# Attention and an MLP mixer on one core: block transposes that read with a step, per-unit moves, and row 0 written by the same list as the other rows

## The chip, the core and the metric

The kernel runs on one core of a Trainium2 chip. The core has five engines that run side by side, each through its own instruction stream in order: TensorE (PE, matrix products, with its weight loads shown apart as PEld), VectorE (DVE), ScalarE (ACT), GpSimd (POOL) and SyncE (SP). They meet only at semaphores. Data moves by DMA; a transfer is issued by an instruction in the queue of one of the engines (here SP's and ScalarE's), carried by 16 DMA engines, and counted as landed when its semaphore is raised. Matrix products land in PSUM, which has eight banks; everything else lives in SBUF, 128 partitions wide.

The metric is the device time of one execution in microseconds (us), the median of several runs.

## The reference

Eight batch rows, eight heads, 576 tokens, head size 64. All arithmetic is in float32. The four weight matrices come as float64 and the kernel turns them into float32 itself.

```python
scores = scale * np.matmul(q, k.transpose(0, 1, 3, 2))
thresh = np.max(scores, axis=-1, keepdims=True) - tau
scores = np.where(scores >= thresh, scores, -1000000000.0)
attn = np.exp(scores - np.max(scores, axis=-1, keepdims=True))
attn = attn / (np.sum(attn, axis=-1, keepdims=True) + 1e-09)
out = np.matmul(attn, v)                       # heads side by side: x is (8, 576, 512)
h = np.maximum(x.transpose(0, 2, 1) @ w_tok1, 0.0) @ w_tok2      # token products, 576 -> 256 -> 576
u = x + h.transpose(0, 2, 1)
return u + np.maximum(u @ w_ch1, 0.0) @ w_ch2                    # channel products, 512 -> 1536 -> 512
```

## The kernel before

**Units and groups.** Attention of a batch row is done for pairs of heads (`p`), two pairs at a time, in 18 units of 128 query rows (`units`; nine units cover two pairs, and unit 4 of the nine takes 64 rows of each, `SHARED`). For a unit, `scores` are products of 128 queries with 576 keys, for two heads. VectorE takes the maximum (`top`, L859), GpSimd makes a bias of it (`shift`, L864), ScalarE cuts what is below the threshold (`mask`, L874, an activation out of PSUM) and takes exponentials with their sum (`exps`, L884), VectorE inverts the sum (`inverse`, L337 and L338), GpSimd scales (`scale`, L345). Then the weights `e` (128 queries by 1152 keys of two heads) must be turned, since the product with v contracts over keys. Three units make a group (`GU`), and one call of `values` (L425, L430) does the product for a group into one PSUM bank, which is copied to `xT`.

**Turning e, rows 1 to 7.** VectorE's transpose works on blocks of 32 x 32. `turn_blocks` (L382) turns a unit's blocks into a part of the tile `T`, one `T` for a group, two in rotation: block row i of the queries stays in partitions 32i to 32i+31, and the four blocks a of every 128 keys lie side by side. `move` then brings block (i, a) from partitions 32i.. to partitions 32a.. by DMA from SP's queue (L392): for each a four transfers, each of 32 partitions for three units at once, 16 transfers for a group, issued when all three units are turned. **u** (the residual input of the channel products) is turned in the same manner for the final addition: `turn_u` (L937) and `move_u` (L944), 16 transfers for a group of 256 tokens; the put-off groups do so too (`Late.turn_u`, L1274 and L1280).

**Turning e, row 0.** TensorE turns 128 x 128 pieces against an identity (`turn`, L363), nine for a unit in three thirds, and VectorE (thirds 0 and 2) or ScalarE (third 1) copies them out of PSUM (`turned`, L369).

**MLP.** A row's token products come in steps x (turn back, L459 and L463), 1 (L471) and 2 (L483, with the sum on VectorE in L493), then channel products for a group of 256 tokens: `ch1` (L950), `ch2` (L966), addition and store. Row 0 does two such groups, rows 1 to 6 one, and what is left of each row is written to DRAM (`spill`, L535) and done at the end in five joined groups (`Late`, L1285), with seven products in place of eight; six sums of weights (`sums`, L1206 and L1209) are made for these on VectorE.

**Order of the work.** Row 0 is a loop written out by hand (`for u in range(UB)`): in each turn the scores of a unit, a value group or an early token step, the scaling of the unit before, a portion of the weight conversion (`weight_to`: 31 pieces, each loaded by L192 and passed through ScalarE, VectorE and GpSimd), and the turning of the unit two back. It has PSUM pools of its own (`ps_tr`, `ps_3rd`, `ps_sc`). From row 1 on the order is planned while the program is built: `Scheduler` holds items with an engine, a cost in us, a lag, a rank and dependences, plays them against one clock for each engine, and writes out whichever can start first. Scores come there in rounds of two units (`make_round`, `scores_of_two`, L846) into two tiles of three banks (`ps_s2`); the other two banks (`ps_b`) serve all else. `planned_at` says how much MLP work is to be done before a round's scores. The loads of q and k (`load_qk`, L108; 72 KB each in rows of 128 bytes, eight for a pair) are issued from SP's queue in row 0 and from ScalarE's queue later, into one buffer each (`lq`, `lk`), and turned by `prep` (L294). The end of the attention and of the last row is:

```python
    sched.run(attention_done)
    attn.close()
```

Of the kernel before, what the change touches and what calls it, by code (L numbers as in the profile page):

```python
# [21 lines left out]
def kernel(  # L22
# [55 lines left out]
    row0 = ctx.enter_context(ExitStack())  # L78
    ps_tr = row0.enter_context(tc.tile_pool(name="ps_tr", bufs=2, space=bass.MemoryType.PSUM))
    ps_3rd = row0.enter_context(tc.tile_pool(name="ps_3rd", bufs=1, space=bass.MemoryType.PSUM))  # L80
    ps_sc = row0.enter_context(tc.tile_pool(name="ps_sc", bufs=2, space=bass.MemoryType.PSUM, side="right"))
# [16 lines left out]
    def load_qk(n, eng, parts=range(8), blocks=(range(S // 32),) * 2):  # L98
# [3 lines left out]
        if n not in loaded:  # L102
            loaded[n] = [att.tile([P, S // 32, 32], F32, tag=tag, bufs=1, name=f"{tag}_{n}") for tag in ("lq", "lk")]
# [22 lines left out]
    FIRST = P // 32  # L126
# [4 lines left out]
    load_qk(0, (nc.sync, None), range(0, 8, 2), (range(FIRST, S // 32), None))  # L131
# [49 lines left out]
    def load_piece(i):  # L181
# [7 lines left out]
        if i == len(pieces) - 2:  # L189
            raw_at[i % NRAW] = work.tile([P, NTK * DM], F32, tag="a", bufs=1, name="spare_a").bitcast(U32)  # L190
# [46 lines left out]
    steps_done = 0  # L237

    def weight(n):

        nonlocal steps_done
        for k in range(steps_done, min(steps_done + n, 3 * len(pieces) + 1)):
            i, part = divmod(k, 3)
            if part == 0:
                on_gpsimd(i - 1)
                if i:
                    load_piece(i - 1 + NRAW)
            else:
                on_scalar(i + 1, part - 1)
            on_vector(i, part)  # L250
            steps_done = k + 1

    def weight_to(x):

        weight(max(int(x) - steps_done, 0))

    def need(i):

        weight(3 * i + 4 - steps_done)

    load_piece(0)
    load_v(0)
    for i in range(1, NRAW):
        load_piece(i)
    load_v(1)

# [24 lines left out]
    def scores(u):  # L298
        b, p0, t = units[u]
        sc = [  # L300
            (ps_3rd if b == 0 and (2 * u + h) % 3 == 2 else ps_sc).tile([P, 2, MAIN], F32, tag="sc", name=f"sc{h}_{u}") for h in range(2)
        ]
        if t == SHARED:
            parts = [(b * NP + p0, slice(MAIN, S), slice(0, 64)), (b * NP + p0 + 1, slice(0, LAST), slice(64, P))]
        else:
            o = P * t if t < SHARED else LAST + P * (t - SHARED - 1)
            parts = [(b * NP + p0 + (t > SHARED), slice(o, o + P), slice(0, P))]
        order = [(f, part, h) for f in range(2) for part in parts for h in range(2)]
        for f, (n, cols, rows), h in order if b else sorted(order, key=lambda o: o[2]):
            r = slice(D * h, D * h + D)  # L310
            qT, kT = heads[n]
            nc.tensor.matmul(sc[h][rows, f, 0:HS], lhsT=qT[r, cols], rhs=kT[r, HS * f : HS * f + HS], start=True, stop=True)
        mx = small.tile([P, 2], F32, tag="mx", name=f"mx_{u}")
        bias = small.tile([P, 2], F32, tag="bias", name=f"bias_{u}")
        for h in range(2):
            c = slice(h, h + 1)
            nc.vector.tensor_reduce(out=mx[:, c], in_=sc[h][:, :, 0:HS], axis=AX.XY, op=ALU.max)
            nc.gpsimd.tensor_scalar(out=bias[:, c], in0=mx[:, c], scalar1=toff, scalar2=-SCALE, op0=ALU.add, op1=ALU.mult)
        st[u] = sc, bias
# [28 lines left out]
    def small_bank(name):  # L348
        return ps_tr.tile([P, MAIN], F32, tag="tr", name=name)
# [1114 lines left out]
```

## Time and profile before

| | us |
|---|---|
| median of 3 runs (1387.57 to 1390.39) | 1389.01 |
| the profiled execution: time | 1385.2 |
| the profiled execution: span, first to last instruction | 1383.4 |
| TensorE busy (mean granted clock 0.965) | 1264.3 |
| VectorE busy | 780.9 |
| ScalarE busy | 563.9 |
| GpSimd busy | 371.5 |
| row 0's first channel product (L950) starts | 165.5 |
| last conversion on GpSimd (L231) starts | 177.9 |
| attention of the last row ends on TensorE | 959.5 |

A "busy" figure is the time in which the engine had an instruction at work. A wait is written as *engine tile line <- who ended it: us in total, times, longest*. An instruction list of a line gives count, shortest, median and longest duration in ns, and first and last start. Letters after an engine (SPq, ACTq) mean its instruction queue, where DMA issues stand. Idle time of an engine that isn't the bound costs nothing by itself.

### The profile page before, as it was taken

What the parts mean: (1) busy time and instruction counts of PE and PEld (TensorE: products, weight loads), DVE (VectorE), ACT (ScalarE), POOL (GpSimd) and SP (SyncE); (2) the same over time, 40 slices, a digit from 0 to 9 for tenths busy, and PEclk for the clock granted to TensorE, in tenths of its full rate; (3) what the DMA queues carried; (4) which work ended last, traced back from release to release, by engine and by line L of the source; (5) the groups of instructions that cost most, each with busy time, mean ns of one, the idle gap of its engine ahead of it and who ended that gap; (6) DMA issues with size and microseconds to landing.
All of it is one profiled execution on the core that took longest, in us unless ns stands there. A gap on an engine that the chain in (4) does not pass through costs nothing.

```text
span 1383.4 us, 21958 instructions
## 1 busy us (share of the span) xinstructions
PE 1264.3 (91%) x7902; PEld 1003.6 (73%) x7902; DVE 780.9 (56%) x1422; ACT 563.9 (41%) x1208; POOL 371.5 (27%) x710
## 2 busy tenths in 40 slices
PE   7882899989898899899989899998999999999998
PEld 5552677758675676775777587676698888888887
DVE  5877866664455755665666566663334344434342
ACT  6775655564544545545544545462011111102020
POOL 4565533333133332333323233330000001010100
PEclk7995999999999999999999999999899999999999
DMA  6436677762777665767666666665011110121011
GB/s 112 108 89 154 165 142 150 134 132 71 155 154 152 141 130 125 166 131 148 137 135 129 136 146 129 138 142 127 1 56 29 59 30 28 32 61 31 31 31 31
DMA packets 310589, 145.15 MB, mean 105 GB/s; under 512 B 210064, under 2 KB 303248, under 8 KB 310480
## 3 DMA queue, kind: packets, MB, share of 16 engines
q1 hardware_dynamic: 182768, 127.84, 40.3%
q10 hardware_dynamic: 127712, 15.90, 8.0%
q8 instruction: 63, 1.03, 0.3%
q14 instruction: 46, 0.38, 0.1%
HBM read 47.32 MB, written 13.50 MB: 44 GB/s over the span
## 4 chain that ended last, share of the span: by engine, by line
PE 59%; DMA 13%; DVE 10%; SPq 10%; ACT 4%; issue 2%; POOL 1%; ACTq 1%; DVEq 0%; POOLq 0%
SPq L392 9%; PE o L1285 9%; PE bank L966 7%; DMA eT<-T 6%; PE sc L846 6%; PE hx L1285 6%; PE bank L430 5%; PE bank L950 5%; PE hmm L1285 4%; PE oz L1285 4%; PE hz L1285 4%; DVE mx L859 3%; PE bank L483 3%; DMA lk<-in_k_dram 2%; PE bank L471 2%
## 5 line engine op out<-in xcount | busy, mean ns | idle before, releaser
L345 POOL TENSOR_SCALAR e<-e,rr 128x576 f32<-128x576 f32 x288 | 213.7, 755 | 303.1 <-DVE rr L338 270.6
L874 ACT ACTIVATE e<-sc,bias 128x576 f32<-128x576 f32 x252 | 173.6, 740 | 237.0 <-DVE mx L859 119.4
L859 DVE TENSOR_REDUCE mx<-sc 128x1 f32<-128x576 f32 x252 | 173.9, 748 | 61.9 <-PE sc L846 61.2
L382 DVE STREAM_TRANSPOSE T<-e 128x1152 f32<-128x1152 f32 x126 | 171.2, 1364 | 41.4 <-POOL e L345 19.9
L884 ACT ACTIVATE e<-e,ntau 128x576 f32<-128x576 f32 x252 | 193.0, 777 | 0.8
L950 PE MATMUL bank<-xT,wc 128*128 128x256 f32 x768 | 178.9, 389 | 12.6 <-DVE x_sb L463 7.2
L966 PEld LDWEIGHTS bank<-wc,g 128*128 128x128 f32 x1536 | 175.4, 192 | 8.5 <-issue 3.6
L966 PE MATMUL bank<-wc,g 128*128 128x128 f32 x1536 | 179.8, 276 | 0.2 <-ACT x_sb L463 0.2
L950 PEld LDWEIGHTS bank<-xT,wc 128*128 128x128 f32 x768 | 145.1, 193 | 42.8 <-issue 7.5
L846 PE MATMUL sc<-kT,qT 64*128 64x192 f32 (+1 forms) x1680 | 146.9, 335 | 12.2 <-ACT e L874 12.0
L846 PEld LDWEIGHTS sc<-kT,qT 64*128 64x128 f32 (+1 forms) x1680 | 122.3, 178 | 39.4 <-issue 18.4
L430 PE MATMUL bank<-eT,lv 128*64 128x384 f32 (+1 forms) x912 | 130.6, 430 | 0.0
L1368 POOL TENSOR_TENSOR us<-us,ut 128x256 f32<-128x256 f32 x27 | 22.4, 843 | 401.8 <-DVE us L1206 401.8
L430 PEld LDWEIGHTS bank<-eT,lv 128*64 128x64 f32 x912 | 76.6, 148 | 45.7 <-issue 31.6
L864 POOL TENSOR_SCALAR bias<-mx,toff 128x1 f32<-128x1 f32 x252 | 66.4, 268 | 152.6 <-DVE mx L859 149.2
L483 PE MATMUL bank<-w,a 128*128 128x288 f32 x256 | 70.9, 424 | 12.8 <-DVE xT L493 10.2
L425 PE MATMUL bank<-eT,vl 128*64 128x384 f32 (+1 forms) x228 | 43.8, 462 | 39.6 <-DMA eT<-T 17.5
L483 PEld LDWEIGHTS bank<-w,a 128*128 128x128 f32 x256 | 47.4, 193 | 33.2 <-DVE xT L493 14.6
L471 PE MATMUL bank<-x_sb,w 128*128 128x512 f32 (+1 forms) x170 | 70.8, 567 | 0.5 <-ACT x_sb L463 0.5
L1206 DVE TENSOR_TENSOR temps<-hx,temps 128x256 f32<-128x256 f32 x60 | 25.5, 425 | 63.5 <-PE hx L1285 63.4
L1333 ACT ACTIVATE ga<-hmm 128x256 f32<-128x256 f32 x30 | 11.5, 384 | 117.0 <-PE hmm L1285 117.0
L1285 PE MATMUL hx<-t,wc 128*128 128x256 f32 x240 | 56.7, 379 | 0.0
(147 smaller groups left out, 1685.8 us busy)
## 6 DMA issues: line engine op xcount, KB each, us to landing
eT<-T SPq DMA_DIRECT2D x672, 108.0 KB, 2.4
lv<-in_v_dram SPq DMA_DIRECT2D x32, 288.0 KB, 3.8
out_dram<-us SPq DMA_DIRECT2D x32, 256.0 KB, 2.1
ut<-us SPq DMA_DIRECT2D x256, 32.0 KB, 1.9
lk<-in_k_dram ACTq DMA_DIRECT2D x109, 72.0 KB, 3.3
lq<-in_q_dram ACTq DMA_DIRECT2D x106, 72.0 KB, 2.9
spare<-in_moe_w_ch_dram SPq DMA_DIRECT2D x8, 512.0 KB, 3.8
extra<-in_moe_w_ch_dram SPq DMA_DIRECT2D x8, 512.0 KB, 3.7
```

Source lines behind the costliest of these rows:

```text
L345: nc.gpsimd.tensor_scalar(out=eh, in0=eh, scalar1=rr[:, h : h + 1], scalar2=1.0, op0=ALU.mult, op1=ALU.mult)
L382: nc.vector.transpose(out=T[:, :, place, :].rearrange("p a (c x) -> p c a x", c=NK), in_=e.rearrange("p (c a x) -> p c a x", c=NK, a=4))
L392: nc.sync.dma_start(out=turned_e[key][32 * a : 32 * a + 32, :, i, :], in_=Ts[key][32 * i : 32 * i + 32, a, :, :])
L430: nc.tensor.matmul(to[r], lhsT=lv[:, j, :], rhs=e[j], start=False, stop=(c == NI - 1), skip_group_check=True)
L483: nc.tensor.matmul(bank[:, 0:HS], lhsT=hidden[b][:, m, P * c : P * c + P], rhs=w2[:, m, HS * f : HS * f + HS], start=(m == 0), stop=(m == ...
L846: nc.tensor.matmul(sc[h][rows, f, HT * k : HT * k + HT], lhsT=qT[r, cols], rhs=kT[r, HT * f : HT * f + HT], start=True, stop=True, skip_gr ...
L859: nc.vector.tensor_reduce(out=mx[:, h : h + 1], in_=part[h], axis=AX.XY, op=ALU.max)
L874: nc.scalar.activation(out=eh, in_=part[h], func=AF.Prelu, bias=bias[:, h : h + 1], scale=SCALE, alpha=STEEP)
L884: nc.scalar.activation(out=eh, in_=eh, func=AF.Exp, bias=ntau, accum_out=rs[:, h : h + 1])
L950: nc.tensor.matmul(bank[:, 0:n], lhsT=wc1[:, j, c, :], rhs=uT[:, c, GR * i : GR * i + n], start=(c == 0), stop=(c == NCC - 1))
L966: nc.tensor.matmul(to, lhsT=s["g"][:, j, P * t : P * t + P], rhs=wc2[:, j, P * c : P * c + P], start=(j == 0 and b > 0), stop=(j == NJ - 1 ...
L1285: nc.tensor.matmul(ps, lhsT=l, rhs=r, start=start and x == 0, stop=x == len(pairs) - 1, skip_group_check=not start)
```

## The change

It has three parts.

*Transposes with a step.* VectorE's transpose of a unit now reads, out of every 128 keys, the keys 4r + a (r from 0 to 31) as its block a, where it read the 32 keys from 32a on. After the transpose partition 32i + r holds, for query block i, all four a side by side, which are the keys 4r + a; and so one transfer can bring the 32 partitions of a query block to all 128 partitions of `eT`. There are four transfers for a unit, each 144 KB, issued for every unit by itself; `T` belongs to a unit and has three buffers. `u` is treated in the same way, in the rows (two transfers for each of four blocks) and in the put-off groups (eight for each half).

*Row 0 by the list.* The loop is gone, with its PSUM pools; row 0's units are made by `make_round` like all others, in rounds of two, with the turning by TensorE in three thirds as items of the list. The weight conversion becomes a set of items (`make_conversion`), and so do the token steps of row 0's first half (`make_half_row`).

*Costs and buffers.* Nearly all item costs, ranks and lags get new numbers. Items on SP's queue get a model of transfers: eight in flight, a rate, a landing time. All loads of q and k after the first move to SP's queue, with two buffers; `e` has four buffers, not three; one spare conversion buffer gets a place of its own.

```diff
-            loaded[n] = [att.tile([P, S // 32, 32], F32, tag=tag, bufs=1, name=f"{tag}_{n}") for tag in ("lq", "lk")]
+            loaded[n] = [att.tile([P, S // 32, 32], F32, tag=tag, bufs=2, name=f"{tag}_{n}") for tag in ("lq", "lk")]
...
-            Ts[key] = att.tile([P, 4, GU, NK * 32], F32, tag="T", name=f"T_{u}")
-        T = Ts[key]
-        nc.vector.transpose(
-            out=T[:, :, place, :].rearrange("p a (c x) -> p c a x", c=NK), in_=e.rearrange("p (c a x) -> p c a x", c=NK, a=4)
-        )
+        T = Ts[u] = att.tile([P, 4, NK * 32], F32, tag="T", bufs=3, name=f"T_{u}")
+        nc.vector.transpose(
+            out=T.rearrange("p a (c x) -> p c a x", c=NK), in_=e.rearrange("p (c r a) -> p c a r", c=NK, a=4)
+        )
...
         for i in range(4):
-            nc.sync.dma_start(out=turned_e[key][32 * a : 32 * a + 32, :, i, :], in_=Ts[key][32 * i : 32 * i + 32, a, :, :])
+            nc.sync.dma_start(
+                out=turned_e[key][:, place, i, :], in_=T[32 * i : 32 * i + 32]
+            )
...
-    for u in range(UB):
-        _, p0, t = units[u]
...
-        scores(u)
...
+    FLIGHT, RATE, LANDING = 8, 214.0, 1.5
...
+            if x.dmas and len(self.in_flight) == FLIGHT:
+                t = max(t, self.in_flight[0])
...
-                put(("load", n, lo), sched.op("act", 0.9, lambda lo=lo: load_qk(n, (nc.scalar,) * 2, range(lo, lo + 2)), ahead, 3, lag=3.0))
...
+                    sched.op(
+                        "sp",
+                        0.9,
+                        lambda lo=lo: load_qk(n, (nc.sync,) * 2, range(lo, lo + 2)),
+                        ahead,
+                        0,
+                        after=(key_op("load", n - 1, LOADS - 2),),
+                        dmas=(2, 107, 0.45),
+                    ),
...
-            e = att.tile([P, 2 * S], F32, tag="e", bufs=3, name=f"e_{u}")
+            e = att.tile([P, 2 * S], F32, tag="e", bufs=4, name=f"e_{u}")
...
-        us = (UB + 2 * it, UB + 2 * it + 1)
+        us = (2 * it, 2 * it + 1)
...
-        x.plan = planned_at(row, k)
+        x.plan = planned_at(row - 1, k) if row else -1.0
...
-            if t % GU == 0:
-                deps += [key_op("M", G - 2, a) for a in range(4)] if G >= 2 else [key_op("V", G - 2)]
-            deps.append(key_op("T", u - 1))
-            put(("T", u), sched.op("dve", 1.37, lambda u=u: turn_blocks(u), deps, 4))
+            deps += [key_op("T", u - 1), key_op("M", u - 3)]
+            put(("T", u), sched.op("dve", 1.31, lambda u=u: turn_blocks(u), deps, 4))
+            put(
+                ("M", u),
+                sched.op(
+                    "sp",
+                    2.4,
+                    lambda u=u: move(u),
+                    (key_op("T", u), key_op("V", G - 2) if t % GU == 0 else None),
+                    0,
+                    after=(key_op("M", u - 1),),
+                    dmas=(4, 147, 0.6),
+                ),
+            )
...
-            for a in range(4):
+            for n in range(2):
                 for k in range(4):
-                    nc.sync.dma_start(out=ut[32 * a : 32 * a + 32, :, k, :], in_=us[32 * k : 32 * k + 32, :, a, :])
+                    nc.sync.dma_start(out=ut[:, n, k, :], in_=us[32 * k : 32 * k + 32, n])
```

## The prediction

> **What bounds the kernel now.** First the busy time of the engines in four stretches (columns: stretch and length, then busy time and instructions of matmul, weight load, VectorE, ScalarE and GpSimd, then clock, DMA share, GB/s).
>
> ```profile
> 0.00:165.50 165.50, 117.62 (x683) 78.78 (x684) 125.35 (x247) 110.44 (x225) 91.03 (x147) 0.85 0.53 124
> 165.50:934.00 768.50, 710.74 (x5106) 546.39 (x5105) 478.80 (x850) 390.22 (x834) 255.20 (x533) 0.98 0.67 138
> 934.00:971.00 37.00, 28.78 (x179) 23.37 (x178) 15.60 (x14) 7.26 (x18) 2.93 (x4) 0.94 0.48 118
> 971.00:1384.00 413.00, 407.18 (x1940) 355.05 (x1940) 161.13 (x313) 56.02 (x133) 22.39 (x27) 0.99 0.13 35
> ```
>
> TensorE is the bound from 165.5 us on (92% in the seven rows, 99% in the put-off groups). Its idle time is 47.9 us at the start, 57.8 in the rows, 8.2 at their end, 5.8 in the last stretch: 119.7 us, and only this, the slow clock that goes with it (0.85 at the start) and any TensorE work dropped can be won. The rows take 768.5/7 = 109.8 us each, 101.5 of them TensorE.
>
> Then, where TensorE waits: its list of waits between 173 and 934 us, and its largest wait after 934.
>
> ```profile
> PE bank L425 <- DMA eT<-T: 17.5, 9, 3.6
> PE bank L425 <- DMA ut<-us: 11.3, 3, 6.7
> PE bank L483 <- DVE xT L493: 9.2, 7, 2.5
> PE bank L950 <- DVE xT L434: 3.1, 1, 3.1
> PE bank L425 <- DVE T L382: 3.1, 1, 3.1
> ...
> PE bank L950 <- DVE x_sb L463: 7.2, 1, 7.2
> ```
>
> L425 is the first matmul of a group's values. It waits for the moves of the turned weights (eT<-T, L392); where the wait is put on ut<-us, SP's queue held the u moves between them. That is 28.8 us, 31.9 with the one on L382, of the row stage's 57.8. The timeline of SP's queue shows the two sharing one line (start, length, instruction):
>
> ```profile
> 359.87 20.58 SPq L392 DMA_DIRECT2D eT<-T  x24
> 380.49 5.08 SPq L944 DMA_DIRECT2D ut<-us  x8
> ...
> 571.31 14.61 SPq L392 DMA_DIRECT2D eT<-T  x16
> ```
>
> One issue takes 598 ns where nothing holds it (instruction list of L392), so sixteen take 9.6 us at best and here 14.6, then 2.4 us to land. Last, ScalarE's waits after 165 us, and the turning instruction:
>
> ```profile
> ACT e L874 <- DMA lk<-in_k_dram: 31.2, 6, 6.7
> ACT e L874 <- DMA lq<-in_q_dram: 22.8, 5, 5.5
> ...
> L382 DVE STREAM_TRANSPOSE T<-e x126: 1334/1369/1380, 144.0 to 940.6; 128x1152 f32<-128x1152 f32 x126
> ```
>
> The q and k loads stand in ScalarE's own queue, and it is held 54 us by them.
>
> **The change, step by step, against the profiled execution (span 1383.4, time 1385.2, so 1.8 around it).** The result is quoted as a median: before's, 1389.0, is 3.8 above the profiled execution, and I add that at the end.
>
> *Moves of e.* 672 issues become 504 (12 for three units, not 16): 168 x 0.598 = 100 us less of SP's queue. The path gets shorter by more than that: after the third unit's transpose there were 16 issues (9.6 us) before the last landing; now units 1 and 2 have gone ahead and 4 remain (2.4 us): 7.2 us earlier, 42 times. Bytes are alike (672 x 108 KB and 504 x 144 KB, 72.6 MB), so the DMA engines win nothing. A shape of 144 KB over 128 partitions isn't in the trace; its landing lies between the 2.4 us of eT (108 KB) and the 3.8 us of lv (288 KB); I take 2.6. The longest wait on these moves is 3.6 us and a wait on ut 6.7, all at or under 7.2, so up to all 31.9 us could go; what is late next is the scaling on GpSimd and L382 itself, and the list starts values earlier where it believes the moves are. I take two thirds, 20 us; bounds 5 (the list only shifts its order) and 32.
>
> *Moves of u.* 96 become 48 in the rows: 8 x 0.595 = 4.8 us less per group, already in the 31.9. The 160 late ones become 80; TensorE is 99% busy there: nothing, the cover is the whole channel phase between transpose and first use.
>
> *Transposes that read with a step.* 126 of L382 now read every fourth element. The bottom is the row's minimum, 1.33 us. No row reads at that step: L223 reads every second word in 691 ns for 512, while contiguous two-input L1209 takes 683, so a step of two is free. Upper end: twice, 2.74 us (an estimate; step four touches twice the length of step two). I take 1.37, nearest to L223, cost nothing: VectorE is busy 68.4 of 109.8 us per row. At 2.74 it would have 93 of 109.8.
> The Trainium skill ("SBUF — State Buffer", section "Door 1: The DMA port swizzle") says memory lines are 16 bytes, that two hits per line are wanted and each access crossing to a new line pays; four fp32 are exactly one line, so it speaks against this read. L223 stays at two hits per line, so no run here shows it. By that rule the transposes would sit towards 2.74 and the sum would lose some 30 us; by the row, none.
>
> *q and k loads from ScalarE's queue to SP's, with two buffers.* 215 issues at 320 to 483 ns leave ScalarE, and its 54 us of waits with them. SP gets 32 a row, 13 us. SP per row: before 96 x 0.598 + 16 x 0.595 x 6/7 + 4 x 0.48 = 67 us plus stores; after 72 x 0.598 + 4.1 + 13 + 1.9 = 62. So its load is no larger, but now moves queue behind loads. Gain on TensorE: of named waits, only 0.9 us on L846 <- ACT: zero, bound -54 (rival 2) to +4.
> By "DMA: Bandwidth & Descriptors", section "Issuing engines are not separate DMA queues", the two queues end on the same 16 DMA engines and a second only saves issue time; that agrees with no gain in transfer, and puts the price on SP alone.
>
> *Row 0 by the list.* In the changed kernel's order of instructions, before row 0's first channel matmul (at 165.5 us in the trace, L950) TensorE gets four rounds of row 1, not three, and the weight conversion ends inside row 0's units. ScalarE's work until there: 25 units x (2 x 0.740 + 2 x 0.977) = 86, 31 pieces x 2 x 0.6 = 37, 26 copies of eT x 0.479 = 12, others 5: 140 us. VectorE: 26 x 2 x 0.748 = 39, conversion 44, copies 28 x 0.55 = 15, preps 12 x 0.75 = 9, reciprocals and the rest 19: 126. Now it is VectorE's 125.4 us in 165.5 (76%). At 90% of ScalarE: 140/0.9 = 156; at 96%, 146; at 80%, 175. I take 90% (TensorE's share in the list's own rows): 10 us gained; bounds -10 and 20. The matmuls of scores in row 0 also change: 31.6 us busy for 18 units (L312) against 146.9/126 x 18 = 21.0 in the form of L846: 10.6 us less TensorE work, but it lies where TensorE is idle anyway; I count 2.
>
> *Last row's end.* The 7.2 us before L950: two x_sb copies stood on VectorE behind six weight sums of 1.76 us (L1206, L1209). In the changed kernel's order all of that row's copies are on ScalarE. Gain 6; bounds 0 and 7.
>
> *Clock.* In the rows the mean is 0.98; after a wait of 3.6 us four matmuls of L425 took 1.55 us, not 0.87. Shorter waits give some of the lost 2% of 711 us back: 3; bounds 0 and 10.
>
> *Item costs and SP's model in the list* have no time of their own; they change which order is written, and are in the two thirds above.
>
> **Sum**: 20 + 10 + 2 + 6 + 3 = 41; span 1383.4 - 41 = 1342, time 1344, median **1348**.
>
> **Rivals.**
> 1. *The moves are hidden anyway, and row 0 gains little.* For: TensorE is at 92%, and a list that plans values earlier may just wait on VectorE's xT sums (L483, 9.2 us) or on evictions instead. Against: 28.8 us of waits carry the moves' name. Then 5 + 0 + 2 + 6 = 13 us, or 23 with the start's 10: median 1366 to 1376.
> 2. *Slower: SP's queue becomes the wait.* Place: a load of q or k at the head of SP's queue, waiting for its buffer or behind a store that waits for its sums, with moves behind it. For: 11 waits of 4.9 us on these loads hit ScalarE now. Price: up to 54 us on values. Against: two buffers let loads run a pair ahead. It decides when over 41 of these 54 us reach TensorE with the 20 us of the moves lost too, from 21 us: 30 to 45 us on TensorE gives 1383.4 - 21 + 30..45, median 1398 to 1413.
> 3. *Slower: step-four transposes at half rate.* 18 x 1.37 = 24.7 us more VectorE a row, to 85%; it becomes the bound outright only above 1.37 + (101.5 - 68.4)/18 = 3.2 us. Before that each value group is 1.4 us later and evictions queue: 4 to 8 us a row against 41 gained: median 1376 to 1404.
> 4. *No change in all:* the gains meet a row 0 that runs at 80%: about 1389.
>
> **How the numbers follow.** Forecast 0.50 (1328 to 1362: start at its bounds, moves 10 to 32); rival 1 0.27; rival 2 0.12; rival 3 0.08, half of it slower; rival 4 0.03. The measurement of before spreads 1387.57 to 1390.39, so 0.2% (2.8 us) is about what can be told. Faster 0.50 + 0.27 + 0.04 (rival 3's milder half) = 0.81; slower 0.12 + 0.04 = 0.16; same 0.03. Range 1324 to 1398: it holds the forecast, rival 1 and the milder half of the slower ones.
>
> **What would show it.** Right: L425's waits on eT<-T under 10 us in the rows, no wait over 2 us on u's moves; ScalarE's waits on lk and lq gone; L382 still at 1.37 us; row 0's first channel matmul near 156 us; no 7 us hole before the last row's token products; row stage near 745 us. Wrong: SP issues of moves waiting behind loads, L382 over 1.8 us, TensorE idle at the start over 50 us, or a new wait on scaling or evictions that takes the place of the moves'.

## The result, and the profile after

| | us |
|---|---|
| before, median of 4 runs (1386.25 to 1390.39) | 1388.29 |
| after, median of 4 runs (1365.39 to 1372.79) | 1369.74 |
| ratio, with its 95% interval | 0.986 (0.983 to 0.990) |
| forecast | 1348, range 1324 to 1398 |
| profiled execution after: span / time | 1367.7 / 1369.5 |
| TensorE busy / VectorE busy after (before: 1264.3 / 780.9) | 1263.7 / 906.2 |

The changed kernel is 18.6 us (1.4%) faster. The forecast was a gain of 41: the sign is right, the size less than half, and the time lies in the range. The parts hide much larger numbers than their sum: one part loses 51 us and the others win 69.

The first view is the busy time of the engines in the four stretches that the prediction read, now of the changed kernel (stretch and length, busy time and instructions of matmul, weight load, VectorE, ScalarE and GpSimd, then clock, DMA share, GB/s).

```profile
0.00:165.50 165.50, 124.51 (x804) 87.89 (x806) 149.40 (x263) 123.03 (x253) 97.47 (x159) 0.88 0.67 149
165.50:934.00 768.50, 711.20 (x5115) 542.18 (x5111) 577.05 (x823) 381.85 (x829) 248.46 (x524) 0.99 0.60 134
934.00:971.00 37.00, 36.16 (x163) 25.95 (x162) 18.87 (x21) 6.87 (x15) 0.00 (x0) 1.00 0.27 77
971.00:1368.00 397.00, 391.85 (x1908) 346.99 (x1906) 160.87 (x299) 56.37 (x135) 22.41 (x27) 1.00 0.13 36
```

TensorE now idles 41.0 us in the first stretch (47.9 before), 57.3 in the rows (57.8) and 0.8 at their end (8.2). So the start and the end gained 7 us each, and the rows nothing: TensorE is still 711 us busy in 768.5. VectorE's busy time in the rows rose by 98 us, with fewer instructions than before (823, 850 before). The cause is one line of the instruction list, the transposes of e (count, shortest, median and longest in ns, first and last start):

```profile
L299 DVE STREAM_TRANSPOSE T<-e x126: 2185/2296/2404, 142.4 to 931.5; 128x1152 f32<-128x1152 f32 x126
```

The same elements took 1369 ns before. The list of TensorE's waits between 173 and 934 us (engine, tile, line, who ended it, us in total, times, longest) shows what took the place of the old ones:

```profile
PE bank L402 <- DVE xT L412: 21.9, 10, 3.6
PE bank L817 <- DVE g L825: 8.2, 6, 2.7
PE sc L712 <- ACT e L740: 4.3, 6, 1.4
PE bank L817 <- DVE xT L353: 3.1, 2, 2.9
```

Of before's 28.8 us of waits of the first values product on the moves, 1.0 us is left under the moves' own name, and 2.4 us under that of a load of q, which now stands in the same queue as the moves. Most of the waits are now on VectorE: on the sums of xT (L412; 9.2 us before), on the relu (L825) and on the copies out of PSUM (L353). From 165 to 940 us all waits that end with VectorE add to 42 us, and all waits to 58. What such a wait looks like stands in the timeline of the changed kernel around 705 us (start, length, instruction; in brackets the idle time ahead of it and who ended it):

```profile
703.24 4.46 DVE L299 STREAM_TRANSPOSE T<-e 128x1152 f32<-128x1152 f32 x2
...
703.76 1.99 PE L817 MATMUL bank<-xT,wc 128*128 128x256 f32 x8
...
707.87 0.60 DVE L353 COPY xT<-bank 128x192 f32<-128x192 f32 x2
...
708.62 0.67 PE L817 MATMUL bank<-xT,wc 128*128 128x256 f32 x2 [2.87 <-DVE xT L353]
```

Two transposes stand on VectorE ahead of the copies that free TensorE's bank. The list reckoned 1.31 us for each (`sched.op("dve", 1.31, ... turn_blocks(u))`), 2.62 for the pair; they took 4.46. TensorE finished what it had at 705.75 and stood 2.87 us.

### The profile page after: what moved, and what is told of

It is laid out like the page before. It is cut to its first block, busy times and chain, and to the rows that moved or that the text cites. A ratio compares the mean times of both kernels' runs of the same rounds, so it can differ in the third digit from the quotient of the medians.

```text
span 1367.7 us, 21924 instructions
## 1 busy us (share of the span) xinstructions
PE 1263.7 (92%) x7982; PEld 1003.0 (73%) x7982; DVE 906.2 (66%) x1405; ACT 568.1 (42%) x1231; POOL 368.3 (27%) x710
## 4 chain that ended last, share of the span: by engine, by line
PE 53%; DVE 21%; SPq 7%; ACT 6%; DMA 5%; issue 5%; POOL 1%; DVEq 0%; ACTq 0%; POOLq 0%
PE o L1175 9%; DVE T L299 8%; PE bank L833 6%; DVE mx L725 6%; PE hx L1175 6%; PE bank L817 6%; SPq L311 5%; PE sc L712 4%; PE hz L1175 4%; PE oz L1175 4%; PE hmm L1175 4%; PE bank L349 4%; ACT e L740 3%; ACT e L750 2%; PE bank L390 2%
## 5 line engine op out<-in xcount | busy, mean ns | idle before, releaser
L740 ACT ACTIVATE e<-sc,bias 128x576 f32<-128x576 f32 x288 | 197.9, 741 | 266.8 <-DVE mx L725 195.4
L299 DVE STREAM_TRANSPOSE T<-e 128x1152 f32<-128x1152 f32 x126 | 286.2, 2292 | 34.0 <-DMA eT<-T 20.5
L725 DVE TENSOR_REDUCE mx<-sc 128x1 f32<-128x576 f32 x288 | 198.1, 746 | 42.7 <-PE sc L712 42.6
L750 ACT ACTIVATE e<-e,ntau 128x576 f32<-128x576 f32 x288 | 220.9, 780 | 0.2
L712 PE MATMUL sc<-kT,qT 64*128 64x192 f32 (+1 forms) x1920 | 178.4, 347 | 21.5 <-ACT e L740 21.2
L712 PEld LDWEIGHTS sc<-kT,qT 64*128 64x128 f32 (+1 forms) x1920 | 147.1, 185 | 52.9 <-ACT e L740 29.0
L730 POOL TENSOR_SCALAR bias<-mx,toff 128x1 f32<-128x1 f32 x288 | 77.5, 273 | 238.2 <-DVE mx L725 236.2
L349 PE MATMUL bank<-eT,lv 128*64 128x384 f32 (+1 forms) x1024 | 135.8, 407 | 0.0
L402 PE MATMUL bank<-w,a 128*128 128x288 f32 x256 | 74.0, 436 | 23.5 <-DVE xT L412 21.9
L261 DVE TENSOR_SCALAR rr<-rs 128x2 f32<-128x2 f32 x144 | 43.7, 304 | 74.1 <-ACT e L750 73.6
L390 PEld LDWEIGHTS bank<-x_sb,w 128*128 128x128 f32 x180 | 34.8, 198 | 34.0 <-issue 28.6
```

The costliest lines, as they stand in the source:

```text
L299: nc.vector.transpose(out=T.rearrange("p a (c x) -> p c a x", c=NK), in_=e.rearrange("p (c r a) -> p c a r", c=NK, a=4))
L349: nc.tensor.matmul(to[r], lhsT=lv[:, j, :], rhs=e[j], start=False, stop=(c == NI - 1), skip_group_check=True)
L390: nc.tensor.matmul(bank[:, 0 : P * L], lhsT=w1[:, t, P * m : P * m + P], rhs=x_sb[:, t, cols], start=(t == 0), stop=(t == NT - 1))
L402: nc.tensor.matmul(bank[:, 0:HS], lhsT=hidden[b][:, m, P * c : P * c + P], rhs=w2[:, m, HS * f : HS * f + HS], start=(m == 0), stop=(m == ...
L712: nc.tensor.matmul(sc[h][rows, f, HT * k : HT * k + HT], lhsT=qT[r, cols], rhs=kT[r, HT * f : HT * f + HT], start=True, stop=True, skip_gr ...
L725: nc.vector.tensor_reduce(out=mx[:, h : h + 1], in_=part[h], axis=AX.XY, op=ALU.max)
```

## The experiments

Theories. **A**: the read with a step makes each transpose 0.93 us longer, and this work on VectorE is what was lost. **B**: the moves were hidden anyway, so the part meant as the gain has little to give. **C**: the longer transposes would fit, but the list, which writes the order of all engines, was told 1.31 us, and a plan made with a price that is too low makes TensorE wait for VectorE. Every run is compared with runs of the kernel before on the same chip, 1385.1 to 1387.3 us in median. Medians of four runs, ratio to before with its 95% interval.

### What the read with a step costs

In the changed kernel (`plain_read`), and the reverse in the kernel before (`before_step`):

```diff
 plain_read, against after
-            out=T.rearrange("p a (c x) -> p c a x", c=NK), in_=e.rearrange("p (c r a) -> p c a r", c=NK, a=4)
+            out=T.rearrange("p a (c x) -> p c a x", c=NK), in_=e.rearrange("p (c a r) -> p c a r", c=NK, a=4)
 before_step, against before
-            out=T[:, :, place, :].rearrange("p a (c x) -> p c a x", c=NK), in_=e.rearrange("p (c a x) -> p c a x", c=NK, a=4)
+            out=T[:, :, place, :].rearrange("p a (c x) -> p c a x", c=NK), in_=e.rearrange("p (c x a) -> p c a x", c=NK, a=4)
```

> The changed kernel with one thing undone: the transposes of e read 32 neighbouring keys as before, all else (four transfers a unit, list, costs) as it is. The keys then meet other keys' values, so the output is another one; the work is the same. Theory A, that the read with a step (2.30 us for each of 126, not 1.37) took what the shorter moves gave: the transpose falls back to 1.37 us, VectorE loses 117 us of busy time, the waits of L402 on the sums in L412 (21.9 us) and of L817 on VectorE (13 us) shrink by more than half, and the time falls by 15 to 28 us, to 1342 to 1355. Theory B, that the list's order and the evictions would hold the rows anyway: VectorE is at 75% of the row stage and the time falls by less than 6 us, to 1364 or above.

> The kernel before with the read of the transposes of e alone changed, to every fourth key; its moves, its list and its costs stay, so the keys meet other keys' values and the output is another one. Theory A: the transposes go from 1.37 to 2.30 us here too, 117 us more of VectorE, and the time rises by 10 to 30 us over 1388, to 1398 to 1418. Theory B: VectorE has room in the rows (68 of 110 us), under 6 us more.

Measured: `plain_read` **1318.3** (0.951, 0.949 to 0.953), so the read with a step cost the changed kernel 51 us, and all else that the change does won 69. `before_step` **1414.0** (1.020, 1.016 to 1.023): the same read costs the kernel before 27 us. There the list was told 1.37 us, and the group line of VectorE (busy and mean ns, idle ahead of it and who ended it) has

```profile
L382 DVE STREAM_TRANSPOSE T<-e 128x1152 f32<-128x1152 f32 x126 | 285.7, 2285 | 40.4 <-DMA eT<-T 22.4 <-POOL e L345 16.7 <-issue 0.7
```

`before_step` lies in the range that theory A gave; for `plain_read` it had expected 28 us at most. So a gain was there and was lost again, and B is no account of the small result. How much of the gain came from the moves themselves this pair doesn't say; that follows below. The duration of one transpose, 2.29 us against 1.37, is the same in both kernels.

### The work, or the order planned for it

The kernel's code is the changed kernel's, with two other costs told to the list. The list then writes another order. It also chooses by these costs, for copies and relus out of PSUM that carry a second engine (`other` in the code), whether VectorE or ScalarE does them:

```diff
 price_told, against after
-            put(("T", u), sched.op("dve", 1.31, lambda u=u: turn_blocks(u), deps, 4))
+            put(("T", u), sched.op("dve", 2.24, lambda u=u: turn_blocks(u), deps, 4))
-                turn = sched.op("dve", 1.2, turn_u, have + state["stores"] + state["adds"] + (converted if b == 1 else []), 5)
+                turn = sched.op("dve", 2.1, turn_u, have + state["stores"] + state["adds"] + (converted if b == 1 else []), 5)
```

> The changed kernel with the list told what the transposes cost: 2.24 instead of 1.31 us for e, 2.1 instead of 1.2 for u; the instructions are the same, only their order changes. Theory C, that the wrong price made the order bad: the time falls by 5 to 15 us, to 1355 to 1365. Theory A, that it is VectorE's work itself: within 5 us of 1369.7, and the waits on VectorE stay above 25 us.

> The changed kernel with the list told halfway between the changed kernel's price and the real one: 1.78 us for e's transpose, 1.65 for u's two. Theory C: the loss of 41 us comes from each unit that VectorE is late by; if it grows with the error, half the error costs half, 1345 to 1353; if the list's own slack takes up a small error, 1328 to 1335 (a step between 1.78 and 1.31); if any error of this kind upsets the order, 1362 or more.

> The changed kernel with a price above the real one: 2.6 us for e's transpose (2.30 real), 2.4 for u's two. With the plain read a price 0.87 too high did no harm (1315 against 1318). So 1322 to 1330 here; if the true price is best, 1332 or more.

> The changed kernel with the list told 3.0 us for e's transpose (2.30 real) and 2.8 for u's two. From 1.31 over 1.78, 2.24 and 2.60 the time fell from 1370 over 1348 and 1328 to 1320. If a price above the real one only adds slack in front of the row maxima, it falls or stays: 1313 to 1322. If the list now plans values later than they could be done, it rises: 1324 or more.

> As the run with 3.0, with 3.6 us for e's transpose and 3.3 for u's two: 1.3 us above the real one, as far as the changed kernel's price is too low by 1.0. If errors of both signs cost alike, some 1360. If only a price that is too low costs, 1315 to 1335.

In the other four the two costs are 1.78 and 1.65, 2.6 and 2.4, 3.0 and 2.8, 3.6 and 3.3.

| told for e's transpose, us (real: 2.30) | median | ratio | span, profiled | TensorE busy | ScalarE's mask waits on the maxima, 165 to 900 us |
|---|---|---|---|---|---|
| 1.31 (the change) | 1369.7 | 0.986 (0.983 to 0.990) | 1367.7 | 1263.7 | 190.3 |
| 1.78 | 1348.1 | 0.973 (0.970 to 0.976) | 1344.7 | 1257.8 | 141.7 |
| 2.24 | 1328.4 | 0.958 (0.956 to 0.960) | 1326.4 | 1252.1 | 128.6 |
| 2.60 | 1320.1 | 0.952 (0.950 to 0.955) | 1318.7 | 1247.9 | 119.0 |
| 3.00 | 1312.5 | 0.947 (0.944 to 0.951) | 1311.5 | 1246.9 | 99.6 |
| 3.60 | 1324.7 | 0.957 (0.952 to 0.961) | 1321.7 | 1249.8 | 69.4 |

C holds: 41 of the 51 us come back by a price alone, where theory C itself had expected 5 to 15. It is a slope, not a step: some 45 us for each us of price up to the real one. Between 1.31 and 2.24 the span falls by 41.3 us, of which 11.6 are TensorE's busy time and 29.7 its idle time. With it goes the clock: between 660 and 900 us the granted clock was 0.96 to 0.97 in the changed kernel and 1.00 with the price told.

The price does two things at once, and no run separates them. It changes the order, and it moves work: with 2.24 told, 13 copies and 16 relus that VectorE did in the changed kernel are ScalarE's. The relus of the channel products on VectorE, in the changed kernel and then in `price_told` (group lines, as above):

```profile
L825 DVE TENSOR_SCALAR g<-bank 128x256 f32<-128x256 f32 x44 | 18.1, 413 | 4.6 <-PE bank L817 4.4
L825 DVE TENSOR_SCALAR g<-bank 128x256 f32<-128x256 f32 x28 | 11.8, 421 | 5.8 <-PE bank L817 5.6
```

In all VectorE has 1405 instructions with 1.31 told, 1376 with 2.24, 1363 with 3.0 and 1344 with 3.6, and ScalarE has more by the same numbers. Between the first two VectorE's busy time falls by 7.5 us only (906.2 and 898.7), much less than the 41 us. But these copies and relus are among what TensorE waits for (L825 and L353 above), so their place may count for more than their length. TensorE's largest wait, on the sums of xT, which have no second engine in the list, falls from 21.9 to 14.7 us.

What I did not expect is that it goes on past the real price, to 3.0, and turns only then. Errors of the two signs don't cost alike: 1.0 us too low cost 41 against the true price, 1.3 us too high cost nothing against it. With 3.0 TensorE's waits in the rows, 165 to 895 us, are down to these:

```profile
PE bank L402 <- DVE xT L412: 15.9, 11, 2.1
PE bank L378 <- ACT x_sb L382: 2.7, 11, 0.5
PE bank L344 <- DMA eT<-T: 1.9, 1, 1.9
```

This is the fastest version of all that leave nothing of the computation out, **1312.5 us**, 57 us under the changed kernel and 73 under the kernel before, with VectorE busy 888.8 us. That a price above the real one works as slack in front of VectorE's short, urgent items (maxima, copies) fits the last column of the table, but was not tested by itself, and the moved copies and relus are a rival to it. And at 3.6 ScalarE waits least and the time is worse again, so that column alone does not tell the time.

> The changed kernel with the contiguous read of e's transposes (1.37 us of real work; the products then meet other keys' values) but with the list told the price of the read with a step: 2.24 us for e, 2.1 for u. Theory C (what costs is a list that plans with a wrong price): a price that is too high only makes the list plan values later, and keeps VectorE's queue less full than planned; it should lose little against the 1318 of the true price, 0 to 12 us, so 1318 to 1330. If a wrong price costs alike in both directions (some 0.9 us a unit off, as in the changed kernel, which lost 41), it should come near 1350. If the list's order does not matter and only the work does, it comes to 1318 within 3 us, but then the 41 us between the changed kernel and the one with the price told stay without a cause.

The counterpart, contiguous read with the price told as 2.24 and 2.1: **1315.1** (0.950, 0.947 to 0.952), not told apart from the 1318.3 of `plain_read`. So the work that A speaks of, some 110 us more on VectorE (898.7 against 788.9), costs 13 us in the plan made for 2.24 (1328.4 against 1315.1), where it costs 51 in the plan made for 1.31 and 27 in the kernel before: the same work has no one price. The best price found for the read with a step (1312.5) is not slower than either contiguous version; other prices were not tried on those.

### Moves and loads, each alone in the kernel before

Four kernels that keep the old order and costs, row 0's loop included. In the three with new moves the read is contiguous (the products meet other keys' values), so that the step's price is not in them.

```diff
 before_moves, against before
-            nc.sync.dma_start(out=turned_e[key][32 * a : 32 * a + 32, :, i, :], in_=Ts[key][32 * i : 32 * i + 32, a, :, :])
+            nc.sync.dma_start(out=turned_e[key][:, place, i, :], in_=T[32 * i : 32 * i + 32])
...
-        for a in range(4):
-            order = [key_op("M", G - 1, 3) if a == 0 else key_op("M", G, a - 1)]
-            put(("M", G, a), sched.op("sp", 2.5, lambda a=a: move(b, p0, g, a), place + [key_op("V", G - 2)], 0, lag=2.2, after=order))
+            put(("M", u), sched.op("sp", 2.5, lambda u=u: move(u), (key_op("T", u), free), 0, lag=2.2, after=(key_op("M", u - 1),)))
 before_loads, against before
-                put(("load", n, lo), sched.op("act", 0.9, lambda lo=lo: load_qk(n, (nc.scalar,) * 2, range(lo, lo + 2)), ahead, 3, lag=3.0))
+                put(("load", n, lo), sched.op("sp", 0.9, lambda lo=lo: load_qk(n, (nc.sync,) * 2, range(lo, lo + 2)), ahead, 0, lag=3.0, after=(key_op("load", n - 1, LOADS - 2),)))
```

`before_both1` has both edits, `before_both` both and two buffers each for q and k.

> The kernel before, with one part of the change only: the weights of each unit are brought over by four transfers of 144 KB as soon as that unit is turned, three buffers of T, contiguous read (so the products meet other keys' values); u's moves, the loads, row 0 and all costs as before. By the forecast this step is worth 20 us, bounds 5 to 32: 1387 - 20 = 1367, range 1355 to 1382. By rival 1 (the moves are hidden anyway) 5 us or less: 1382 to 1388. If the order that the old costs plan gets worse with it, 1390 or more. The waits of the first values product on the moves, 28.8 us before, should fall under 10 us in the first two cases.

> The kernel before with the loads of q and k from row 1's third pair on issued from SP's queue, one buffer each as before, nothing else. By the forecast this step is worth 0 (bounds -54 to +4): 1386 within 4. Theory D (the loads on ScalarE's queue are held by transfers of SP's queue, because a transfer starts only when the one eight before it in the program has landed, and they hold ScalarE's scores and evictions with them): before's moves come 16 at a time, all ready, so the hold is short there (54 us of ScalarE's waits) and the gain is small, 0 to 15 us: 1371 to 1386. Rival 2 of the forecast (SP's queue becomes the wait): 1395 or more.

> The kernel before with four transfers per unit for the moves (contiguous read, so the products meet other keys' values) and with the loads of q and k on SP's queue, one buffer each. Theory D: the 50 us that the moves alone lost (1437) came from ScalarE being held by its loads, each behind a move that waits for VectorE's transpose; with the loads on SP that is gone and the moves' own gain is seen: 1350 to 1380. If the moves per unit are bad in themselves in this order, it stays at 1420 or more. If single buffers are what holds (loads wait for the preps, moves wait behind them), 1390 to 1420.

> As the run with one buffer, with two buffers for q and for k, loads a pair ahead. Theory D: 1345 to 1375, at most 10 us below the run with one buffer. If the second buffer is what makes the loads harmless on SP's queue, it gains 20 us or more over the run with one buffer.

| | loads on ScalarE's queue | loads on SP's queue |
|---|---|---|
| moves for a group, 16 at a time | 1386 | 1369.6 (0.988, 0.986 to 0.990) |
| moves for a unit, 4 at a time | **1436.8** (1.036, 1.033 to 1.039) | 1360.4 (0.982, 0.979 to 0.985) |

With two buffers 1361.7 (0.982, 0.979 to 0.985): the second buffer does nothing. The moves alone, which I had put at a gain of 20, lose 50; with the loads out of ScalarE's queue they win 9. The loads alone win 17, and 76 once the moves are per unit. The two edits are one: neither can be priced without the other. ScalarE's waits in `before_moves`:

```profile
ACT g L952 <- DMA eT<-T: 31.1, 3, 13.9
...
ACT e L871 <- DMA eT<-T: 24.8, 3, 10.1
...
ACT g L952 <- DMA ut<-us: 19.3, 2, 9.8
```

ScalarE waits here for transfers that it has no use for. The reverse edit in the changed kernel with the price told (`qk_on_act`) makes it plain:

```diff
 qk_on_act, against price_told
-                        "sp",
+                        "act",
-                        lambda lo=lo: load_qk(n, (nc.sync,) * 2, range(lo, lo + 2)),
+                        lambda lo=lo: load_qk(n, (nc.scalar,) * 2, range(lo, lo + 2)),
-                        0,
+                        3,
-                        dmas=(2, 107, 0.45),
+                        lag=3.0,
```

> The changed kernel with the price told (1328), and with the loads of q and k issued from ScalarE's queue again, with two buffers. The forecast took this step at 0 (bounds -54 to +4): 1325 to 1332. If ScalarE's queue was in the way of the scores (54 us of waits on these loads before, 0.38 us of issue time times 250), this costs 5 to 25 us: 1333 to 1353. If SP's queue is the tighter one now (moves wait behind loads), taking 250 issues of some 0.45 us off it gains 3 to 10 us: 1318 to 1325.

Measured: **1446.4** (1.044, 1.041 to 1.046), 118 us more than with the loads on SP's queue, far beyond any of the three expectations. From its timeline around 455 us:

```profile
452.50 7.76 SPq L311 DMA_DIRECT2D eT<-T  x8
452.56 0.51 ACTq L106 DMA_DIRECT2D lq<-in_q_dram  x1
...
455.38 2.32 DVE L299 STREAM_TRANSPOSE T<-e 128x1152 f32<-128x1152 f32 x1
...
457.14 0.32 ACTq L106 DMA_DIRECT2D lk<-in_k_dram  x1
457.50 0.51 ACTq L106 DMA_DIRECT2D lq<-in_q_dram  x1
458.05 0.51 ACTq L106 DMA_DIRECT2D lk<-in_k_dram  x1
458.60 0.53 ACTq L106 DMA_DIRECT2D lq<-in_q_dram  x1
...
463.12 0.32 ACTq L106 DMA_DIRECT2D lk<-in_k_dram  x1
463.56 1.37 ACT L740 ACTIVATE e<-sc,bias 128x576 f32<-128x576 f32 x2 [10.36 <-DMA eT<-T]
```

The instruction lists of the program as built say why an issue waits. Four successive loads on ScalarE, and a move on SP, with the semaphores that each waits for:

```
335 L106 DMACopy lk_2386<-in_k_dram 32x18x32 [waits DMAHW3_49,DMAHW1_49]
336 L106 DMACopy lq_2385<-in_q_dram 32x18x32 [waits DMAHW4_49]
337 L106 DMACopy lk_2386<-in_k_dram 32x18x32 [waits DMAHW5_49]
338 L106 DMACopy lq_2385<-in_q_dram 32x18x32 [waits DMAHW6_49]
...
128 L311 DMACopy eT_2463<-T_2461 128x1x288 [waits DMAHW6_49,DVE_49]
```

The transfers of both queues take eight semaphores in turn (DMAHW0 to 7), and each issue waits for the last transfer that used its own, some eight places before it in the program. A load on ScalarE's queue thus waits for a move on SP's queue; with moves per unit that move may itself still wait for VectorE's transpose. ScalarE takes its instructions in order, so its masks, exponentials and copies stand behind the load: 10.36 us here. On SP's queue the same waits hold only other transfers. The time that ScalarE spends on the issues themselves is no rival for the bulk: nearly the same loads cost 17 us on its queue where the moves come 16 at a time, and 76 with moves per unit. That the eight semaphores are the tie is read from the built program and fits the names that end the waits; a program with more of them was not tried.

### The rest: row 0, the model of SP's queue, the buffers of e

Between `before_both1` (1360.4) and `plain_read` (1318.3) lie 42 us that neither moves nor loads nor the step explain.

```diff
 no_sp_model, against price_told
-            x.other, x.dmas = other, dmas
+            x.other, x.dmas = other, None
+            if dmas:
+                x.lag = 2.5
 e_three, against price_told
-            e = att.tile([P, 2 * S], F32, tag="e", bufs=4, name=f"e_{u}")
+            e = att.tile([P, 2 * S], F32, tag="e", bufs=3, name=f"e_{u}")
-                    deps += [key_op("T", u - 4), key_op("pre", u - 1, 0)]
+                    deps += [key_op("T", u - 3), key_op("pre", u - 1, 0)]
 start_act, against price_told
-                        other=("dve", 0.5, lambda bank, u=u, third=third: turned(u, third, bank, nc.vector.tensor_copy)),
```

> The changed kernel with the price told (1328), and the list's model of transfers taken out: items on SP's queue have their single cost (2.4 us for a unit's moves, 0.9 for two loads) and a landing 2.5 us later, as in the kernel before, in place of eight in flight and a rate. The forecast said that these models have no time of their own: 1326 to 1334. If a good part of the 42 us that lie between the kernel before with moves and loads changed (1360) and the changed kernel with the plain read (1318) is the better plan that this model gives, 1340 to 1365.

> The changed kernel with the price told (1328), with three buffers of e as before, not four. If the fourth buffer is what lets ScalarE run on while VectorE's longer transposes hold e, 1340 to 1370. If it is only room that nobody needs, 1326 to 1333.

> The changed kernel with the price told (1328), and row 0's copies of the turned weights out of PSUM on ScalarE alone, not on whichever engine is free first. In the start VectorE is busy 90 percent until row 0's first channel product at 160 us. If VectorE is what bounds the start, taking its share of these copies (some 0.55 us each) off it brings that product 2 to 8 us earlier, and the time to 1320 to 1327. If ScalarE or the loads bound it (the forecast took ScalarE, 140 us at 90 percent), the copies make it later, 1330 to 1345.

`no_sp_model`: **1354.6** (0.978, 0.974 to 0.981), 26 us lost. Most of it is in row 0: the first channel product starts at 179.7 us there and at 160.2 with the model. The pieces of the weights are loaded by transfers of up to 512 KB, which land 3.9 us after their issue in the changed kernel (median); a fixed landing of 2.5 us may let the list plan the conversion wrongly, but that this is the reason was not tested. Some 16 of the 42 us stay without a named part.

`e_three`: **1326.0** (0.957, 0.954 to 0.959) against 1328.4: the fourth buffer is not needed.

`start_act`: **1329.6** (0.959, 0.956 to 0.961) against 1328.4, not told apart in time. The first channel product came 6.5 us later (166.7 us), as the second expectation had it, with VectorE less busy. The stretch from 120 to 165 us, of `start_act` and then of `price_told`:

```profile
120.00:165.00 45.00, 34.01 (x243) 23.65 (x244) 38.25 (x61) 30.78 (x69) 24.32 (x39) 0.96 0.59 123
```

```profile
120.00:165.00 45.00, 34.75 (x203) 24.24 (x203) 44.13 (x70) 28.87 (x59) 28.29 (x42) 0.89 0.50 131
```

VectorE is at 98% there with the copies and at 85% without; ScalarE is at 64% and 68%, and TensorE is busy alike. So VectorE alone does not bound the start; what does stays open.

### The contiguous read without the wrong keys

If e's blocks are read contiguously, partition 4r + a gets key 32a + r of its 128, so v has to stand in the same order. `v_in_step` loads v so from row 1 on, by four transfers of 72 KB in place of one of 288 KB, and cuts the middle piece by a mask; `v_told` is the same with other prices, of which two are shown.

```diff
 v_in_step, against plain_read
-        nc.sync.dma_start(out=lv, in_=v[b].rearrange("h s d -> (h s) d")[2 * S * p : 2 * S * p + 2 * S, :].rearrange("(c p) d -> p c d", p=P))
+            for a in range(4):
+                nc.sync.dma_start(out=lv[a:P:4], in_=rows.rearrange("(c a r) d -> a r c d", a=4, r=32)[a])
...
+                nc.gpsimd.tensor_scalar(out=vl[:, r], in0=lv[:, NI, :], scalar1=mine[:, h : h + 1], scalar2=1.0, op0=ALU.mult, op1=ALU.mult)
 v_told, against v_in_step
-            put(("T", u), sched.op("dve", 1.31, lambda u=u: turn_blocks(u), deps, 4))
+            put(("T", u), sched.op("dve", 1.37, lambda u=u: turn_blocks(u), deps, 4))
...
-        put(("split", n), sched.op("pool", 0.5, lambda: split_middle(n), (key_op("loadv", n), free), 2))
+        put(("split", n), sched.op("pool", 0.65, lambda: split_middle(n), (key_op("loadv", n), free), 2))
```

> A version that keeps the four transfers and reads neighbouring keys: from row 1 on v is loaded with its rows in the order in which the moves leave the keys (partition 4r + a holds key 32a + r of each 128), by four transfers of 72 KB for a pair in place of one of 288 KB, and the middle piece is split by a mask on all 128 partitions instead of two copies. Theory A: as the plain read, within 5 us: 1342 to 1357, 15 to 25 us under the changed kernel. Theory B: 1364 to 1372; the 84 added issues (0.48 us each, 40 us of SP's queue) could also push moves back by up to 5 us.

> The version that loads v in permuted rows and reads e contiguously (1334), with the list told what its new steps take in its own trace: 0.62 us for each of the four transfers of v (0.5 told before), 0.65 us for the split of the middle piece (0.5), 1.37 us for e's transpose (1.31), 2.1 for u's (1.2). Theory C: what it lost against the 1318 of the plain read is the order, so 1318 to 1327. Rival: it is the transfers themselves (84 more issues on SP, GpSimd waiting 64.5 us on v, not 32.4), then it stays at 1330 to 1338.

`v_in_step`: **1334.4** (0.962, 0.960 to 0.964). It does the whole computation without the step in e's read and is 35 us faster than the change as made, but gives 16 of `plain_read`'s gain back. GpSimd's wait for v, in `v_in_step` and then in `plain_read`:

```profile
POOL vl L329 <- DMA lv<-in_v_dram: 64.5, 18, 15.8
```

```profile
POOL vl L322 <- DMA lv<-in_v_dram: 32.4, 14, 14.2
```

The scaling of e stands behind it on GpSimd. That this wait is what costs the 16 us is not shown. `v_told`: **1345.4** (0.971, 0.969 to 0.974), 11 us *worse* with the traced prices, outside both expectations. So "tell the list what the trace shows" is no rule that always wins; why this order is worse was not found.

## Why the prediction was wrong

**The step that failed is "Transposes that read with a step": "I take 1.37, nearest to L223, cost nothing".** Measured: 2.30 us, between the bounds given (1.33 and 2.74), and 51 us of median, not none. The row that I took it from reads every second word; two words of it still lie within 16 bytes, and the step of four leaves one. The page "SBUF — State Buffer", section "Door 1: The DMA port swizzle", of the Trainium skill had said that each access that crosses to a new 16-byte line pays. The traces of this case agree with that: 691 ns for 512 elements at a step of two, in another instruction; for transposes of 512 elements 1113 ns (in the rows) and 1086 (in the put-off groups) at a step of four, and 622 (half of one of 1024, 1245 ns) and 686 contiguous in the kernel before. The same note also gives 4 fp32 as how far one can stride for free; a step of 4 was not free here. The weight given to it, some 30 us, was nearer than my none. And the step's cost is not in its 0.93 us alone: with that price told to the list, 41 of the 51 us were not lost. A row is a neighbour only if it is on the same side of the rule that speaks against it.

**"VectorE is busy 68.4 of 109.8 us per row", given as cover, holds only for a plan made for it.** Rival 3 reckoned 4 to 8 us a row, 28 to 56 in all, from evictions that queue behind longer transposes; with 51 it was right in size and mechanism, at a chance of 0.08; only its time, 1376 to 1404, was too high, since the other parts won more than 41. It didn't see that the price told to the list was to blame for most of it: with 3.0 us told, the kernel with the same transposes is as fast as the contiguous versions.

**"Moves of e", 20 (5 to 32):** the waits went as forecast, from 28.8 us to 1.0 on the moves of e, with none left on u's, and 2.4 on loads in the same queue. (A move's landing took 2.9 us, where 2.6 was taken.) Worth 9 us by itself where the loads are on SP's queue, minus 50 where they are not. The reading "up to all 31.9 us could go" left out what came next: the waits on the sums of xT went from 9.2 to 21.9.

**"q and k loads", 0 (-54 to +4):** outside the bounds on the side of the gain: 17 us alone, 76 beside per-unit moves. The 54 us of ScalarE's waits were read as harmless because TensorE named ScalarE only for 0.9 us, and the price was put "on SP alone"; the runs put it on ScalarE. The trace before had a sign of it in the same list: the masks waited for moves that they have no use for.

```profile
ACT e L874 <- DMA eT<-T: 11.5, 2, 7.3
```

Rival 2 (SP's queue as the wait) came to no more than the 2.4 us above.

**"Item costs and SP's model in the list have no time of their own":** wrong. The model of SP is worth 26 us, mostly at the start, and one wrong price costs 41.

**"Row 0 by the list", 10 + 2:** TensorE's idle time at the start fell by 6.9 us by the prediction's cut at 165.5, and the first channel product came at 162.1, not 156. 787 matmuls lie before it, not 683; 80 of the 104 more are row 0's scores, 240 smaller products in place of 160, and the rest is about the one more round of row 1 that the prediction counted in. ScalarE, taken as the limit at 90%, was busy 123.0 of 165.5, VectorE 149.4; and `start_act` shows that VectorE is not the limit alone.

**"Last row's end", 6:** the hole is gone; TensorE idles 0.8 us between 934 and 971, where it idled 8.2. **"Clock", 3:** from 0.98 to 0.99 in the rows, but TensorE's busy time there did not fall (710.7 and 711.2 us); in `price_told` its busy time is 12 us less than before over the whole span.

So the sum of 41 was wrong twice, and the errors met: everything but the step won 69, and the step took 51. That the time still lies in the range is luck: two errors of opposite sign.

## What to carry to other kernels

Where a planner writes the order, a cost in it is part of the kernel: when an instruction's access pattern changes, measure it and tell the planner; a price too low by 0.9 us on 126 instructions cost 41 us, and leaning to the high side was safer here. Measure again after it, for in `v_told` true prices made the time worse. A transfer issued from a computing engine holds that engine in order, also for transfers of other queues if they share semaphores; so look at what the issue may wait for before calling its queue free. Price edits together when one changes what the other waits for.

## What the runs showed of the hardware

VectorE's transpose of 128 x 1152 float32 takes 1369 ns with a contiguous read and 2296 ns (1.68 times) with a step of 16 bytes (medians in the two kernels); in the seven plans with this read its mean lies between 2285 and 2322 ns. A step of 8 bytes was seen only in another instruction: 691 ns on 512 elements, where a contiguous one with two inputs took 683. So the price of the 16-byte step is clear, but less than twice.

TensorE's granted clock was lower in stretches with more idle time, but the busy share alone does not tell it. In the kernel with moves alone (420 to 660 us) it was 0.90 to 0.91 where TensorE was busy 86 to 88%. In the version with the price told (420 to 900 us) it was 1.00 at 95% or more. In the changed kernel, however, it was 1.00 at 91 to 92% (420 to 660 us) and 0.96 at 93% (660 to 780 us). What sets it is not shown.
